# Attention decode on one core: the softmax bias moves from POOL to ACT, and PSUM buffers and program order are rearranged

## The chip, the cores and the metric

The kernel runs on 1 core of one Trainium2 chip. The metric is the device time of one execution in microseconds (us), given as the median of several executions. One that takes over 1.5% more than the fastest of its kernel is counted as slow.

Engines: PE is TensorE (PEld its weight loads), DVE is VectorE, ACT is ScalarE, POOL is GpSimd, SP issues the DMAs.

## The reference

Two decode attention blocks, A and B, with one query position, 4 batches, 32 query heads, 8 K/V heads of 128 and a model width of 512. A attends to 4096 keys, B to the last 1024.

```python
q = (x @ wq).reshape(B, Sq, Hq, Dh).transpose(0, 2, 1, 3)
scores = einsum("bhqd,bhkd->bhqk", q, repeat(k, 4)) * (Dh ** -0.5)
p = softmax(scores)
o = einsum("bhqk,bhkd->bhqd", p, repeat(v, 4))
out = o.transpose(0, 2, 1, 3).reshape(B, Sq, Hq * Dh) @ wo
# the results of A and B are concatenated
```

All inputs are bf16. The caches that are used make 84 MB and the weights 17 MB; the core reads 100.67 MB in all.

## The kernel before

The work is cut into 40 units, each with 1 MB of K and 1 MB of V: 32 units for A (one K/V head, one batch, 4096 keys) and 8 for B (one K/V head, four batches, 1024 keys). In a unit

1. PE transposes K in 32 blocks of 128x128 into PSUM, 8 blocks to a bank, and DVE copies each bank to SBUF (K copies);
2. PE makes the scores (32 matmuls with 4 columns), DVE takes the maximum of each partition;
3. POOL takes the maximum over the partitions (an all-reduce, tile bm) and multiplies it by -scale (tile biasT);
4. ACT takes exp(scale * s + biasT); DVE sums each partition, POOL sums over the partitions (an all-reduce, tile den);
5. PE multiplies with V (PV); DVE normalises; after each group of heads PE adds its part of the output projection.

The POOL program before:

```python
for t in range(self.NU):
    ...
    self.wait(g_, f"dve.red.{t}")
    ... g_.partition_all_reduce(self.bm[:, s, 0:w], self.pm[:, s, 0:w], 128, max)
    self.inc(ins, "pool", f"pool.max.{t}")
    self.wait(g_, f"pool.max.{t}")
    ...
    g_.tensor_scalar(out=self.biasT[:, s, 0:w], in0=self.bm[:, s, 0:w],
                     scalar1=-self.scale, scalar2=None, op0=ALU.mult)
    self.inc(ins, "pool", f"pool.bias.{t}")
    if t - self.Ld >= 0:
        self._pool_den(g_, t - self.Ld)     # waits for dve.rsum, all-reduce (add) den<-acc
```

ACT waits for `pool.bias` and for the scores. The order of one step on PE and on DVE, cut to its core:

```python
# PE, step t                         # DVE, step t
transposes(t + 1)                    kcopies(t + LK)        # LK = 2
scores(t)                            reduce_max(t)
pv(t - 2)                            rowsum(t - 1)
outproj(...)                         norm(t - 1)            # waits for pool.den and pv
```

The transposes use two PSUM banks in turn, so group j waits for the K copy of group j - 2. SP issues the loads in program order: K three units ahead of V.

Of the kernel before, what the change touches and what calls it, by code (L numbers as in the profile page):

```python
# [7 lines left out]
ACT_F = mybir.ActivationFunctionType  # L8
ALU = mybir.AluOpType
AX = mybir.AxisListType  # L10

F32 = mybir.dt.float32
# [3 lines left out]
    NK=3,  # L16
# [5 lines left out]
    LT=1,  # L22
    LK=2,
    La=1,
    Ld=1,
    NE=4,
    NY=4,
# [3 lines left out]
    wo1_at=22,  # L31
    KLEAD=3,
)


class _Builder:
    def __init__(self, nc, aps, cfg):
        self.nc = nc
        self.aps = aps
        self.cfg = cfg  # L40
        self.rec = None
        self.NB = 4
        self.DM = 512
        self.HQ = 32
        self.HKV = 8
        self.REP = 4
        self.DH = 128
        self.SK = 4096
        self.W = min(4096, max(256, self.SK // 4))
        self.C = [self.SK // 128, self.W // 128]  # L50
        self.KOFF = [0, self.SK - self.W]
        self.KEYS = [self.SK, self.W]
        self.scale = 1.0 / math.sqrt(float(self.DH))
        self.NK = cfg["NK"]
        self.NV = cfg["NV"]
        self.NRD = cfg["NRD"]
        self.NRA = cfg["NRA"]
        self.NPS = cfg["NPS"]
        self.L = cfg["L"]
        self.LT = cfg["LT"]  # L60
        self.LK = cfg["LK"]
        self.La = cfg["La"]
        self.Ld = cfg["Ld"]
        self.NE = cfg["NE"]
        self.NY = cfg["NY"]
        self.NR = self.NRD + self.NRA
        assert self.L < self.NPS and self.L < self.NE and self.La < self.L and self.Ld <= self.La
        self.LO = max(self.L, self.La + self.LK + 1)
        self.units = []
        for g in range(self.HKV):  # L70
            for b in range(self.NB):
                self.units.append((0, g, b, 1))
        self.NUA = len(self.units)
        for g in range(self.HKV):
            self.units.append((1, g, 0, self.NB))
        self.NU = len(self.units)
        self.Q = 32
        for (P, g, b0, nb) in self.units:
            assert nb * self.C[P] == self.Q
        self.groups = []  # L80
        j = 0
        for t in range(self.NU):
            glist = []
            for q0 in range(0, self.Q, 8):
                glist.append((j, q0, 8))
                j += 1
            self.groups.append(glist)
        self.QB0 = cfg["QB0"]
        assert self.QB0 >= self.L and self.QB0 + self.NPIECE + self.L < self.NUA
# [60 lines left out]
    def _issue_k(self, eng, t):  # L150
        em = self.emit
        P, g, b0, nb, C = self.uinfo(t)
        off = self.KOFF[P]
        r = t % self.NR
        if r >= self.NRD:
            self.wait(eng, "pe.q.0")
        if t - self.NR >= 0:
            self.wait(eng, f"pe.tlast.{t - self.NR}")
        ins = None
        if em:  # L160
            src = self.k_cache[P][b0:b0 + nb, g, off:off + C * 128, :].rearrange(
                "b (p c) d -> p b c d", p=128
            )
            dst = self.Rq(r).rearrange("p (b c) d -> p b c d", b=nb)
            ins = eng.dma_start(dst, src)
        self.op("dma", self.Q * 128 * 128 * 2)
        self.inc(ins, f"dmakr{r}", f"dma.k.{t}", 16)
# [59 lines left out]
    def prog_pool(self, g_):  # L227
# [32 lines left out]
        for t in range(self.NU):  # L260
# [4 lines left out]
            if t - NY >= 0:  # L265
                self.wait(g_, f"pool.bias.{t - NY}")
            ins = (
# [7 lines left out]
            self.inc(ins, "pool", f"pool.max.{t}")  # L275
            self.wait(g_, f"pool.max.{t}")
            if t - NY >= 0:
                self.wait(g_, f"act.exp.{t - NY}.last")
            ins = (
                g_.tensor_scalar(  # L280
                    out=self.biasT[:, s, 0:w], in0=self.bm[:, s, 0:w],
                    scalar1=-self.scale, scalar2=None, op0=ALU.mult,
                )
                if em
                else None
            )
            self.op("pool.tscalar")
            self.inc(ins, "pool", f"pool.bias.{t}")
            if t - self.Ld >= 0:
# [57 lines left out]
    def _act_exps(self, act, i):  # L347
# [5 lines left out]
        kb = i % self.NPS  # L353
        self.wait(act, f"pool.bias.{i}")
        self.wait(act, f"pe.s.{i}")
# [21 lines left out]
    def prog_pe(self, pe):  # L377
# [21 lines left out]
        for step in range(self.NU + LO):  # L399
            t = step  # L400
            if t + LT < self.NU:
                self._pe_transposes(pe, t + LT)
            if t < self.NU:
                self._pe_scores(pe, t)
            i = step - L
            if 0 <= i < self.NU:
                k = step - self.QB0
                if 0 <= k < self.NPIECE:
                    self._pe_qTB_chunk(pe, i, k)
                self._pe_pv(pe, i)  # L410
            i = step - LO
            if 0 <= i < self.NU:
# [24 lines left out]
    def _pe_qTB_chunk(self, pe, i, k):  # L437
        em = self.emit
        ob = i % self.NOT
        self.qb_chunk_of_unit[i] = k  # L440
# [4 lines left out]
        self.wait(pe, "dve.xcopy")  # L445
        if i - self.NOT >= 0:
            self.wait(pe, f"dve.mult.{i - self.NOT}")
        reg = self.oTt[ob][:, 16 + 16 * k:32 + 16 * k].rearrange("p (j bb) -> p j bb", j=4)
        for jj in range(4):
# [17 lines left out]
    def _pe_transposes(self, pe, t):  # L467
        em = self.emit
        P, g, b0, nb, C = self.uinfo(t)
        r = t % self.NR  # L470
        self.wait(pe, f"dma.k.{t}")
        for (j, q0, ng) in self.groups[t]:
            kb = j % 2
            if j - 2 >= 0:
                self.wait(pe, f"dve.kcopy.{j - 2}")
            for k in range(ng):
# [12 lines left out]
    def _pe_scores(self, pe, t):  # L489
# [3 lines left out]
        kb = t % self.NPS  # L493
        self.wait(pe, f"dve.kcopy.{self.groups[t][-1][0]}")
        KTv = self.KTq(s)
        self.wait(pe, f"dve.qcopy.{P}")
        if t - self.NPS >= 0:
            self.wait(pe, f"act.exp.{t - self.NPS}.last")
            self.wait(pe, f"dve.red.{t - self.NPS}")
        ps = self.psT[kb][:, 0:self.Q * 4].rearrange("p (q h) -> p q h", h=4)  # L500
        for b in range(nb):
            qT = self.qT_sb[P][:, b0 + b, self.REP * g:self.REP * g + 4]
            for c in range(C):
                q = b * C + c
                ins = None
                if em:
                    ins = pe.matmul(ps[:, q, :], lhsT=KTv[:, q, :], rhs=qT, start=True, stop=True)  # L507
                self.op("pe.mm4s")
                if q == self.Q - 1:
                    self.inc(ins, "pe_s", f"pe.s.{t}")  # L510

    def _pe_pv(self, pe, i):
# [3 lines left out]
        se = i % self.NE  # L516
        ob = i % self.NOT
        self.wait(pe, f"dma.v.{i}")
        self.wait(pe, f"act.exp.{i}.last")
        if i - self.NOT >= 0:  # L520
            self.wait(pe, f"dve.mult.{i - self.NOT}")
        if i in self.qb_chunk_of_unit:
# [38 lines left out]
    def prog_dve(self, dve):  # L561
# [17 lines left out]
        for step in range(self.NU + La):  # L579
# [3 lines left out]
            if t < self.NU:  # L583
                self._dve_reduce(dve, t)
            i_q = step + LK - self.L - 1
            if i_q in self.qb_chunk_of_unit:
                assert i_q <= step - La, "qT_B chunk copy must precede norm of its unit"
                self._dve_qbcopy(dve, i_q, self.qb_chunk_of_unit[i_q])
# [29 lines left out]
    def _dve_kcopies(self, dve, t):  # L618
        em = self.emit
        P, g, b0, nb, C = self.uinfo(t)  # L620
        s = t % self.NK
        if t - self.NK >= 0:
            self.wait(dve, f"pe.s.{t - self.NK}")
        dst = self.KTq(s)
        for (j, q0, ng) in self.groups[t]:
            kb = j % 2
            self.wait(dve, f"pe.tgrp.{j}")
# [38 lines left out]
    def _dve_qbcopy(self, dve, i, k):  # L666
        em = self.emit
        ob = i % self.NOT
        self.wait(dve, f"pe.qb.{k}")
        ins = None  # L670
        if em:
            ins = dve.tensor_copy(
                self.qT_sb[1][:, :, 4 * k:4 * k + 4].rearrange("p bb j -> p j bb"),
                self.oTt[ob][:, 16 + 16 * k:32 + 16 * k].rearrange("p (j bb) -> p j bb", j=4),
            )
# [5 lines left out]
    def _dve_norm(self, dve, i):  # L681
        em = self.emit
        P, g, b0, nb, C = self.uinfo(i)
        sy = i % self.NY
        ob = i % self.NOT
        w = nb * 4
# [22 lines left out]
    def build(self):  # L709
# [9 lines left out]
        with contextlib.ExitStack() as stack:  # L719
# [29 lines left out]
            self.OT_all = [sb(f"OT_all{P}", [128, self.HQ, self.NB], BF16) for P in range(2)]  # L749
            self.out_sb = sb("out_sb", [128, 2, self.DM], BF16)  # L750
            self.psT = [pb(f"psT{k}", [128, 512], F32) for k in range(self.NPS)]
            self.NOT = 8 - self.NPS - 3
            assert self.NOT >= 1
            self.oTt = [pb(f"oT{k}", [128, 512], F32) for k in range(self.NOT)]
            self.oT = [t[:, 0:16] for t in self.oTt]
            self.outp = pb("outp", [128, self.DM], F32)
            self.KTps_t = [pb(f"KTps{k}", [128, 512], F32) for k in range(2)]
            self.KTps = [t[:, :].bitcast(BF16).rearrange("p (c k) -> p c k", c=8)
# [14 lines left out]
            names += [f"dmav{s}" for s in range(NV)]  # L773
            names += [f"dmakr{r}" for r in range(NRD + NRA)]
            for n in names:
                self._new_sem(n)
# [83 lines left out]
```

## Time and profile before

| | before |
|---|---|
| median of 15 runs | 802.79 us (799.23 to 806.29) |
| span of the profiled run | 805.4 us |
| busiest compute engine | PE, 31% of the span |
| DMA queue | 33.7% of 16 engines' span |
| POOL, idle on "issue" before biasT and den | 332.3 + 236.3 us |

Part 1 of the profile page of the kernel before is the busy time of each engine, with its share of the span:

```profile
PE 248.5 (31%) x4168; PEld 213.9 (27%) x4168; DVE 137.3 (17%) x332; ACT 50.1 (6%) x257; POOL 44.5 (6%) x128
```

No engine is anywhere near full. Such a page suggests that something waits in series, and one has to look for who waits for whom. The view of the waits (engine and line that waits, releaser, us in total, times, longest):

```profile
ACT e_sb L365 <- POOL biasT L280: 716.4, 40, 22.3
DVE rden L692 <- POOL den L304: 601.3, 40, 25.1
PE KTps L479 <- DVE KT L630: 490.6, 37, 23.6
```

ACT and DVE wait for POOL, PE waits for DVE. POOL is the head of the queue although it is busy for only 6%. The groups of POOL instructions tell the rest (busy us, mean ns of one, then the idle time just before them and what ended it):

```profile
L304 POOL PARTITION_ALL_REDUCE den<-acc x40 | 17.7, 442 | 237.1 <-issue 236.3 <-DVE acc L662 0.8
L268 POOL PARTITION_ALL_REDUCE bm<-pm x40 | 15.4, 385 | 177.5 <-DVE pm L646 169.4 <-issue 8.1
L280 POOL TENSOR_SCALAR biasT<-bm 128x4 f32<-128x4 f32 (+1 forms) x40 | 10.5, 263 | 332.3 <-issue 332.3
```

"issue" is idle time in which the engine waited for nothing that the profile shows. POOL stands still for 568.6 us before biasT and den, with no other engine to blame. In order of time it looks like this (start, us, engine, line, instruction, idle before it):

```profile
319.07 0.44 POOL L304 PARTITION_ALL_REDUCE den<-acc  x1 [5.84 <-issue]
323.49 0.38 POOL L268 PARTITION_ALL_REDUCE bm<-pm  x1 [3.98 <-DVE pm L646]
331.47 0.26 POOL L280 TENSOR_SCALAR biasT<-bm 128x4 f32<-128x4 f32 x1 [7.60 <-issue]
337.70 0.44 POOL L304 PARTITION_ALL_REDUCE den<-acc  x1 [5.97 <-issue]
...
798.38 0.44 POOL L304 PARTITION_ALL_REDUCE den<-acc  x1 [5.93 <-issue]
799.61 0.44 POOL L304 PARTITION_ALL_REDUCE den<-acc  x1 [0.79 <-DVE acc L662]
```

The all-reduce bm follows another all-reduce and starts as soon as DVE is done. The tensor_scalar, which follows an all-reduce, and the all-reduce den, which follows the tensor_scalar, have 6 to 8 us of nothing before them. The last two den follow each other with no multiply between them, and the gap is not there.

### The profile page before, as it was taken

What the parts mean: (1) busy time and instruction counts of PE and PEld (TensorE: products, weight loads), DVE (VectorE), ACT (ScalarE), POOL (GpSimd) and SP (SyncE); (2) the same over time, 40 slices, a digit from 0 to 9 for tenths busy, and PEclk for the clock granted to TensorE, in tenths of its full rate; (3) what the DMA queues carried; (4) which work ended last, traced back from release to release, by engine and by line L of the source; (5) the groups of instructions that cost most, each with busy time, mean ns of one, the idle gap of its engine ahead of it and who ended that gap; (6) DMA issues with size and microseconds to landing.
All of it is one profiled execution on the core that took longest, in us unless ns stands there. A gap on an engine that the chain in (4) does not pass through costs nothing.

```text
span 805.4 us, 9583 instructions
## 1 busy us (share of the span) xinstructions
PE 248.5 (31%) x4168; PEld 213.9 (27%) x4168; DVE 137.3 (17%) x332; ACT 50.1 (6%) x257; POOL 44.5 (6%) x128
## 2 busy tenths in 40 slices
PE   1712222322232224333322332232223222333323
PEld 1712222222222223332222222222222222222201
DVE  0501111111111112211111111111111111111100
ACT  0000000000000000000000000000000001112111
POOL 0000000000000000000000000000000000000000
PEclk9955555555555555555555555555555555555555
DMA  8995444332222222222523333433233221110000
GB/s 354 392 407 189 172 171 169 131 104 106 105 105 105 105 105 105 105 105 91 205 106 137 133 142 135 142 110 111 99 127 110 107 78 52 53 53 1 1 1 1
DMA packets 27867, 101.31 MB, mean 126 GB/s; under 512 B 1696, under 2 KB 9904, under 8 KB 19120
## 3 DMA queue, kind: packets, MB, share of 16 engines
q1 hardware_dynamic: 27824, 100.69, 33.7%
q8 instruction: 33, 0.54, 0.3%
q14 instruction: 10, 0.08, 0.0%
HBM read 100.67 MB, written 0.01 MB: 125 GB/s over the span
## 4 chain that ended last, share of the span: by engine, by line
issue 88%; POOL 5%; PE 3%; DMA 2%; DVE 1%; POOLq 1%; SPq 0%; ACT 0%
POOL den L304 2%; POOL bm L268 2%; DMA rawKd<-in_A_k_cache_dram 2%; PE KTps L479 2%; POOL biasT L280 1%; PE outp L550 0%; PE psT L426 0%; DVE KT L630 0%; POOLq L280 0%; POOLq L304 0%; PE psT L507 0%; ACT e_sb L365 0%; DVE out_sb L614 0%; DVE rden L692 0%; DVE pm L646 0%
## 5 line engine op out<-in xcount | busy, mean ns | idle before, releaser
L479 PE MATMUL KTps<-ident,rawKd 128*128 128x128 bf16 x896 | 103.2, 307 | 325.0 <-DVE KT L630 317.3
L479 PEld LDWEIGHTS KTps<-ident,rawKd 128*128 128x128 bf16 x896 | 88.9, 143 | 339.3 <-DVE KT L630 324.3
L630 DVE COPY KT<-KTps 128x1024 bf16<-128x1024 bf16 x160 | 106.7, 686 | 36.9 <-PE KTps L479 36.6
L692 DVE RECIPROCAL rden<-den 128x4 f32<-128x4 f32 (+1 forms) x40 | 7.7, 193 | 601.3 <-POOL den L304 601.3
L479 PE MATMUL KTps<-ident,big_w 128*128 128x128 bf16 x384 | 45.1, 312 | 173.3 <-DVE KT L630 173.3
L365 ACT ACTIVATE e_sb<-psT,biasT 128x32 bf16<-128x32 f32 (+1 forms) x256 | 48.8, 329 | 716.4 <-POOL biasT L280 716.4
L479 PEld LDWEIGHTS KTps<-ident,big_w 128*128 128x128 bf16 x384 | 39.0, 145 | 178.2 <-DVE KT L630 176.5
L529 PE MATMUL oT<-e_sb,V 128*128 128x4 bf16 x1280 | 39.7, 166 | 45.8 <-ACT e_sb L365 42.5
L529 PEld LDWEIGHTS oT<-e_sb,V 128*128 128x128 bf16 x1280 | 37.3, 104 | 48.1 <-issue 48.1
L507 PEld LDWEIGHTS psT<-qT_sb,KT 128*128 128x128 bf16 x1280 | 41.9, 106 | 0.9 <-issue 0.9
L507 PE MATMUL psT<-qT_sb,KT 128*128 128x4 bf16 x1280 | 41.3, 167 | 0.0
L304 POOL PARTITION_ALL_REDUCE den<-acc x40 | 17.7, 442 | 237.1 <-issue 236.3
L280 POOL TENSOR_SCALAR biasT<-bm 128x4 f32<-128x4 f32 (+1 forms) x40 | 10.5, 263 | 332.3 <-issue 332.3
L268 POOL PARTITION_ALL_REDUCE bm<-pm x40 | 15.4, 385 | 177.5 <-DVE pm L646 169.4
L550 PE MATMUL outp<-big_w,OT_all 128*4 128x512 bf16 x32 | 14.8, 622 | 1.4 <-DVE OT_all L699 1.4
L550 PE MATMUL outp<-wo_sb,OT_all 128*4 128x512 bf16 x32 | 14.9, 620 | 0.0
L662 DVE TENSOR_REDUCE acc<-e_sb 128x4 f32<-128x128 bf16 (+1 forms) x40 | 11.1, 277 | 9.3 <-ACT e_sb L365 9.3
L646 DVE TENSOR_REDUCE pm<-psT 128x4 f32<-128x128 f32 (+1 forms) x40 | 11.2, 281 | 0.0
L699 DVE TENSOR_TENSOR OT_all<-oT,rden 128x4 bf16<-128x4 f32 (+1 forms) x40 | 6.9, 173 | 1.4
L550 PEld LDWEIGHTS outp<-big_w,OT_all 128*4 128x4 bf16 x32 | 2.9, 108 | 7.8 <-issue 5.1
L454 PE MATMUL oT<-xT_sb,big_w 128*128 128x4 bf16 x128 | 4.5, 166 | 0.0
L454 PEld LDWEIGHTS oT<-xT_sb,big_w 128*128 128x128 bf16 x128 | 4.0, 104 | 0.0
(18 smaller groups left out, 17.1 us busy)
## 6 DMA issues: line engine op xcount, KB each, us to landing
V<-in_A_v_cache_dram SPq DMA_DIRECT2D x32, 1024.0 KB, 5.1
rawKd<-in_A_k_cache_dram SPq DMA_DIRECT2D x22, 1024.0 KB, 8.3
big_w<-in_A_k_cache_dram SPq DMA_DIRECT2D x10, 1024.0 KB, 7.7
V<-in_B_v_cache_dram SPq DMA_DIRECT2D x8, 1024.0 KB, 5.3
rawKd<-in_B_k_cache_dram SPq DMA_DIRECT2D x6, 1024.0 KB, 7.7
big_w<-in_A_wq_dram SPq DMA_DIRECT2D x1, 4096.0 KB, 12.5
big_w<-in_B_wq_dram SPq DMA_DIRECT2D x8, 512.0 KB, 12.3
wo_sb<-in_A_wo_dram SPq DMA_DIRECT2D x8, 512.0 KB, 10.9
```

Source lines behind the costliest of these rows:

```text
L268: g_.partition_all_reduce(self.bm[:, s, 0:w], self.pm[:, s, 0:w], 128, bass.bass_isa.ReduceOp.max)
L280: g_.tensor_scalar(out=self.biasT[:, s, 0:w], in0=self.bm[:, s, 0:w], scalar1=-self.scale, scalar2=None, op0=ALU.mult,)
L304: g_.partition_all_reduce(self.den[:, s, 0:w], self.acc[:, s, 0:w], 128, bass.bass_isa.ReduceOp.add)
L365: ins = act.activation(self.e_sb[:, se, b * C:(b + 1) * C, h], ps[:, b * C:(b + 1) * C, h], ACT_F.Exp, bias=self.biasT[:, sy, idx:idx + 1] ...
L454: ins = pe.matmul(reg[:, jj, :], lhsT=self.wq_sb[1][:, kc, j * 128:(j + 1) * 128], rhs=self.xT_sb[:, 1, kc, :], start=(kc == 0), stop=(kc ...
L479: ins = pe.transpose(self.KTps[kb][:, k, :], self.Rq(r)[:, q0 + k, :], self.ident128[:, :],)
L507: ins = pe.matmul(ps[:, q, :], lhsT=KTv[:, q, :], rhs=qT, start=True, stop=True)
L529: ins = pe.matmul(self.oT[ob][:, b * 4:(b + 1) * 4], lhsT=self.Vq(s)[:, q, :], rhs=self.e_sb[:, se, q, :], start=(c == 0), stop=(c == C - 1),)
L550: ins = pe.matmul(self.outp[0:self.NB, :], lhsT=self.OT_all[P][:, h, :], rhs=self.wo_sb[P][:, h, :], start=(h == 0), stop=(h == self.HQ - 1),)
L630: ins = dve.tensor_copy(dst[:, q0:q0 + ng, :], self.KTps[kb][:, 0:ng, :])
L646: ins = dve.reduce_max(self.pm[:, sy, 0:w], ps, axis=AX.X)
L662: ins = dve.reduce_sum(self.acc[:, sy, 0:w], ev, axis=AX.X)
```

## The change

The diff has four intents: to take the multiply off POOL and give it to ACT; to double the PSUM banks of the transposes (two to four), paid for by putting the PV result into spare columns of the score banks; to run PV before the scores and K copies one unit ahead instead of two; and to prepare a path that lets the DMA transpose K, which is left empty (`XBAR_UNITS=()`). The core of the diff:

```diff
-    LK=2,
+    LK=1,
+    NKTB=4,
+    XBAR_UNITS=(),
 ... POOL program
-            self.wait(g_, f"pool.max.{t}")
-            ...
-                g_.tensor_scalar(
-                    out=self.biasT[:, s, 0:w], in0=self.bm[:, s, 0:w],
-                    scalar1=-self.scale, scalar2=None, op0=ALU.mult,
-                )
-            self.inc(ins, "pool", f"pool.bias.{t}")
 ... ACT program
-        self.wait(act, f"pool.bias.{i}")
+        self.wait(act, f"pool.max.{i}")
+            act.activation(
+                self.biasT[:, sy, 0:nb * 4], self.bm[:, sy, 0:nb * 4],
+                ACT_F.Copy, scale=-self.scale,
+            )
+        self.inc(ins, "act", f"act.bias.{i}")
+        self.wait(act, f"act.bias.{i}")
 ... PE program: the scores move behind PV
-            if t < self.NU:
-                self._pe_scores(pe, t)
             i = step - L
             if 0 <= i < self.NU:
                 ...
                 self._pe_pv(pe, i)
+            if t < self.NU:
+                self._pe_scores(pe, t)
 ... transposes
-            kb = j % 2
-            if j - 2 >= 0:
-                self.wait(pe, f"dve.kcopy.{j - 2}")
+            kb = j % self.NKTB
+            if j - self.NKTB >= 0:
+                self.wait(pe, f"dve.kcopy.{j - self.NKTB}")
 ... PSUM
-            self.oTt = [pb(f"oT{k}", [128, 512], F32) for k in range(self.NOT)]
-            self.oT = [t[:, 0:16] for t in self.oTt]
+            self.oT = [t[:, 128:144] for t in self.psT]
 ... (the waits and the q_B columns that follow from this are cut)
```

## The prediction

> **What bounds the kernel now.** No engine is busy over 31% of the span (page, part 1: PE 248.5 us, DVE 137.3, ACT 50.1, POOL 44.5 of 805.4); the DMA queue has 33.7% (part 3). The chain of waits is 88% "issue", between POOL instructions. The groups of instructions show where: before the 40 tensor_scalar (biasT) POOL idles 332.3 us on "issue", 8.3 us each, and before the all-reduces den 236.3 us, 6.1 us each, though their inputs are ready. Before the all-reduce bm there is no such gap (timeline: it starts 0.1 us after the row maximum it waits for), and the last two all-reduces den follow each other without one. So an all-reduce is really 0.4 us, and the gap appears where POOL changes between the all-reduce and an ordinary instruction, both ways. [...] the other direction costs more, 11 us while DMA is full. A unit takes 17.6 to 20 us; 14.4 of it are these two changes.
>
> **What the change does.** The -scale multiply moves from POOL to ACT. POOL then runs only all-reduces: both changes go, 569 us, all on the chain. ACT gets 40 small activations, an estimated 0.2 to 0.3 us each (an exp is 0.22); ACT has 0.87 us of work in an A unit and 2.64 in a B unit, so this is off the path. I expect no further table loads.
> The rest (four transpose buffers, LK=1, oT in the score banks, PV before scores) frees PE from waiting on DVE copies two groups back. The cross-bar path is empty and does nothing.
>
> **What bounds it then.** 805 - 569 = 236 us is below two floors:
> - DMA: 100.69 MB. Windows with a full queue show 393 to 428 GB/s; at 400, 252 us, plus a slow first 5 us and a tail of about 8 us: 262 to 268.
> - PE: 248.5 us at mostly half clock, starting at 17 us, plus the tail: 271, more with gaps. An A unit is 3.8 (32 transposes at 118 ns) + 1.04 + 0.99 + 0.47 = 6.3 us at half clock against 5.2 us of DMA. At 32 us the trace shows transposes at 66 ns after dense PE work; then a unit is about 4.3 us and DMA bounds. [...]
> - DVE: 3.7 us a unit, below both.
>
> Early units also carry 8.4 MB of weights, so are DMA-bound; later ones start PE-bound and should warm the clock. I expect 272 us, range 257 to 300.
>
> **What would show it.** POOL "issue" idle gone (under 20 us in all), all-reduces still 0.38 to 0.44 us; DMA share 9 tenths in most slices, 380 to 410 GB/s; PE mean clock well above 0.54; a unit every 5.2 to 6.3 us; PE's largest waits on K or V loads, not on DVE.
>
> **What would make it wrong.** The gap could belong to each all-reduce, or max and add could need different code: about 6 us a unit would stay, 450 us or more. Copy and Exp could alternate table loads (1.28 us each): up to 100 us on ACT, partly hidden. The clock could stay at half and PE, DVE and POOL hand over in series: 300 us or more. [...]
>
> Chances: faster by over 2% 0.98, within 2% 0.01, slower 0.01.

Two phrases have these numbers in the trace of the kernel before: in the "slow first 5 us" the queue moved 154 GB/s, against 418 in the next 5; and that later units "should warm the clock" is the author's estimate from the transposes, which took 66 ns each at 32.7 us, behind dense PE work, and 117 ns each at 46.5 us, at a granted clock of 0.50.

## The result, and the profile after

The changed kernel takes 269.54 us (median of 8 runs, 268.27 to 270.02), against 802.79 us. The ratio is 0.3356, with a 95% interval of 0.3349 to 0.3363. Ratios here are the mean time of one kernel's fast runs over that of the other's of the same rounds, so they are not quite the ratio of the medians.

Part 1 of the page, two rows of part 2 (the span in 40 slices: granted PE clock and busy DMA, in tenths) and the DMA queue of part 3, of the changed kernel:

```profile
PE 218.1 (81%) x4168; PEld 191.1 (71%) x4168; DVE 130.4 (49%) x332; ACT 58.3 (22%) x297; POOL 32.6 (12%) x88
...
PEclk9997997757755557757555756897797777759956
DMA  6999999999999999999999999999999999999810
...
q1 hardware_dynamic: 27824, 100.69, 95.3%
```

The DMA queue, 33.7% before, is now full in 36 consecutive slices. PE does the same 4168 matmuls in less busy time; its mean granted clock rose from 0.536 to 0.733 in the two profiled runs.

The groups of POOL instructions of the changed kernel, and then a stretch of its POOL timeline:

```profile
L319 POOL PARTITION_ALL_REDUCE den<-acc x40 | 19.6, 489 | 24.2 <-DVE acc L692 24.2
L296 POOL PARTITION_ALL_REDUCE bm<-pm x40 | 15.0, 374 | 196.7 <-DVE pm L676 196.7
```

```profile
158.85 0.37 POOL L296 PARTITION_ALL_REDUCE bm<-pm  x1 [4.34 <-DVE pm L676]
159.13 0.50 POOL L319 PARTITION_ALL_REDUCE den<-acc  x1
163.99 0.37 POOL L296 PARTITION_ALL_REDUCE bm<-pm  x1 [4.36 <-DVE pm L676]
```

"issue" is gone before both all-reduces; POOL now waits for DVE, as it should. The all-reduces last about as long as before (bm 374 ns against 385, den 489 against 442). A unit takes about 5 us, 163.99 - 158.85 = 5.14 here. What ACT got, in its groups:

```profile
L371 ACT ACTIVATE biasT<-bm 128x4 f32<-128x4 f32 (+1 forms) x40 | 8.4, 210 | 200.7 <-POOL bm L296 200.7
L371 ACT ACT_TABLE_LOAD x1 | 1.3, 1283 | 0.7 <-PEq L876 0.7
```

The multiply costs ACT 8.4 us in all. There is still one table load in the whole program (1.28 us): Copy beside Exp causes none. The waits of PE in the changed kernel:

```profile
PE KTps L505 <- DMA rawKd<-in_A_k_cache_dram: 16.2, 5, 7.6
PE KTps L505 <- DMA big_w<-in_A_k_cache_dram: 5.3, 2, 2.8
PE KTps L505 <- DVE KT L660: 5.1, 14, 1.5
```

PE waited 490.6 us for DVE's K copies before. It now waits 5.1 us for them, and most of what is left in these lines is for K loads.

### The profile page after: what moved, and what is told of

Its sections match the earlier page's. It is cut to its first block, busy times and chain, and to the rows that moved or that the text cites. A ratio compares the mean times of both kernels' runs of the same rounds, so it can differ in the third digit from the quotient of the medians.

```text
span 268.2 us, 9433 instructions
## 1 busy us (share of the span) xinstructions
PE 218.1 (81%) x4168; PEld 191.1 (71%) x4168; DVE 130.4 (49%) x332; ACT 58.3 (22%) x297; POOL 32.6 (12%) x88
## 4 chain that ended last, share of the span: by engine, by line
PE 55%; DMA 29%; DVE 7%; SPq 4%; issue 3%; ACT 1%; POOL 0%; DVEq 0%
PE KTps L505 32%; DMA rawKd<-in_A_k_cache_dram 23%; PE psT L558 9%; PE outp L579 6%; DMA big_w<-in_B_k_cache_dram 6%; PE psT L538 5%; DVE KT L660 4%; SPq L210 1%; PE psT L478 1%; PE psT L451 1%; SPq L237 1%; ACT e_sb L390 1%; SPq L251 1%; DVE OT_all L729 1%; DVE qT_sb L702 1%
## 5 line engine op out<-in xcount | busy, mean ns | idle before, releaser
L660 DVE COPY KT<-KTps 128x1024 bf16<-128x1024 bf16 x160 | 99.5, 681 | 9.5 <-PE KTps L505 9.5
L505 PE MATMUL KTps<-ident,rawKd 128*128 128x128 bf16 x896 | 82.7, 272 | 22.6 <-DMA rawKd<-in_A_k_cache_dram 16.2
L505 PEld LDWEIGHTS KTps<-ident,rawKd 128*128 128x128 bf16 x896 | 75.1, 126 | 32.2 <-issue 16.3
L371 ACT ACTIVATE biasT<-bm 128x4 f32<-128x4 f32 (+1 forms) x40 | 8.4, 210 | 200.7 <-POOL bm L296 200.7
L558 PEld LDWEIGHTS psT<-e_sb,V 128*128 128x128 bf16 x1280 | 38.1, 100 | 8.2 <-issue 7.7
L558 PE MATMUL psT<-e_sb,V 128*128 128x4 bf16 x1280 | 39.4, 166 | 5.1 <-DVE acc L692 3.3
L505 PE MATMUL KTps<-ident,big_w 128*128 128x128 bf16 x384 | 36.6, 275 | 7.7 <-DMA big_w<-in_A_k_cache_dram 5.3
L505 PEld LDWEIGHTS KTps<-ident,big_w 128*128 128x128 bf16 x384 | 32.8, 128 | 11.4 <-DMA big_w<-in_A_k_cache_dram 5.4
L538 PEld LDWEIGHTS psT<-qT_sb,KT 128*128 128x128 bf16 x1280 | 36.1, 98 | 3.5 <-issue 3.3
L729 DVE TENSOR_TENSOR OT_all<-psT,rden 128x4 bf16<-128x4 f32 (+1 forms) x40 | 6.9, 174 | 59.3 <-PE psT L558 59.1
```

Of the source, the lines that this page charges most:

```text
L371: act.activation(self.biasT[:, sy, 0:nb * 4], self.bm[:, sy, 0:nb * 4], ACT_F.Copy, scale=-self.scale,)
L505: ins = pe.transpose(self.KTps[kb][:, k, :], self.Rq(r)[:, q0 + k, :], self.ident128[:, :],)
L538: ins = pe.matmul(ps[:, q, :], lhsT=KTv[:, q, :], rhs=qT, start=True, stop=True)
L558: ins = pe.matmul(self.oT[ob][:, b * 4:(b + 1) * 4], lhsT=self.Vq(s)[:, q, :], rhs=self.e_sb[:, se, q, :], start=(c == 0), stop=(c == C - 1),)
L660: ins = dve.tensor_copy(dst[:, q0:q0 + ng, :], self.KTps[kb][:, 0:ng, :])
L729: ins = dve.tensor_tensor(self.OT_all[P][:, self.REP * g:self.REP * g + 4, b0:b0 + nb].rearrange("p h b -> p b h"), self.oT[ob][:, 0:w].re ...
```

## The experiments

Theory A: POOL pays some 6 us or more each time it goes from an all-reduce to the multiply or back, and the whole gain is that these changes are gone. Rivals: the other edits carry part of the gain; the all-reduce itself hides the time; or what cost was the dependence, max, multiply and exp in series through POOL. Theory D: the changed kernel is bound by DMA, not by PE. "Code", which POOL changes or needs in the prediction and the expectations, is the author's guess at what such a gap is; the traces show the gap and its length, not what POOL does in it.

The yardstick was run again in two of the calls: 269.89 us (ratio 0.3334) and 269.79 us (ratio 0.3326). Its ratio moves because the kernel before, on those chips, took 810.7 and 810.37 us. The runs e2 to e6 rest on two executions each, the others on four or five.

> The changed kernel unaltered, as the yardstick for the other runs of this call: 268 to 271 us.

> The changed kernel unaltered, as the yardstick for the other run of this call: 268 to 271 us.

### Only the multiply moves (e1_bias_only)

```diff
 # the kernel before, and of the whole change only this:
-                g_.tensor_scalar(out=self.biasT..., in0=self.bm..., scalar1=-self.scale, ...)
+            act.activation(self.biasT..., self.bm..., ACT_F.Copy, scale=-self.scale)
-        self.wait(act, f"pool.bias.{i}")
+        self.wait(act, f"pool.max.{i}")
```

> The kernel before with only the -scale multiply moved from POOL to ACT (two transpose buffers, LK=2, own oT banks, scores before PV, all as before). Theory A, the whole gain is the two changes of code on POOL: 265 to 300 us, near the changed kernel. Rival B, the other edits (four transpose buffers, order of PV and scores) are needed to use what POOL sets free: over 330 us.

Measured: 271.63 us, ratio 0.3355 (0.3335 to 0.3374); the full change had 0.3334 (0.332 to 0.3348). The moved multiply alone is the gain, to within 2 us. Everything else in the diff is worth 0.6% here by the two ratios, and as their intervals overlap even that is not certain.

### Everything but the multiply (e2_rest_only)

```diff
 # the changed kernel, with the multiply back on POOL
+                g_.tensor_scalar(out=self.biasT..., in0=self.bm..., scalar1=-self.scale, ...)
-            act.activation(self.biasT..., self.bm..., ACT_F.Copy, scale=-self.scale)
```

> The changed kernel with the -scale multiply put back on POOL, all other edits kept. Theory A, the gain is all in the multiply leaving POOL: 770 to 810 us. Rival B, the other edits bring a good part by themselves: under 720 us.

Measured: 750.56 us, ratio 0.9326 (0.9215 to 0.9438). Neither expectation held: the other edits do gain while POOL bounds, 54 us by the medians. The POOL groups of this run:

```profile
L332 POOL PARTITION_ALL_REDUCE den<-acc x40 | 17.7, 442 | 255.0 <-issue 254.3 <-DVE acc L695 0.8
L296 POOL PARTITION_ALL_REDUCE bm<-pm x40 | 15.4, 385 | 144.0 <-DVE pm L679 135.6 <-issue 8.4
L308 POOL TENSOR_SCALAR biasT<-bm 128x4 f32<-128x4 f32 (+1 forms) x40 | 10.5, 263 | 292.7 <-issue 292.7
```

Against the kernel before, POOL waits 169.4 - 135.6 = 33.8 us less for DVE's maximum. From den to the next bm, DVE normalises, copies four K banks and takes the maximum; with two banks it had to wait for PE in the midst of the four copies (3.98 us in the timeline before), with four banks the transposes are already there (3.10 us in the timeline of this run). Another 21.6 us are shorter "issue" (332.3 + 236.3 before, 292.7 + 254.3 here); the spans of the two profiled runs differ by 55.3 us. Why those gaps became shorter was not tested. They vary within a run too: in the kernel before, the one before the tensor_scalar is 10.88 and 11.10 us at 44 and 64 us, while the DMA queue is full (412 and 398 GB/s in these two gaps), and mostly 7 to 9 us later. The gain of these edits and that of the multiply don't add: once POOL is free, DMA bounds, and the 54 us have nowhere to show.

### A multiply that nobody needs (e3_one_scalar, e4_four_scalars)

```diff
 # the changed kernel, in each unit between the two all-reduces; input constant, result unused
+            for k in range(1):          # e4: range(4)
+                g_.tensor_scalar(out=self.scr[:, s, k, 0:4], in0=self.cst[:, 0:4],
+                                 scalar1=-self.scale, scalar2=None, op0=ALU.mult)
```

> The changed kernel plus one tensor_scalar of 128x4 on POOL in each unit, between the two all-reduces; its input is a constant and nobody waits for its result. Theory A, POOL pays for changing between the all-reduce and an ordinary instruction, whatever depends on it: 700 to 810 us, with about 6 us before each following all-reduce and 6 to 9 us before each tensor_scalar. Rival, it was the dependence (max, multiply, exp in series) that cost: 268 to 280 us.

> As the run with one extra tensor_scalar per unit, but four in a row. Theory A, the cost is per change of code: the same gaps once per unit, so at most 35 us (3 x 40 x 0.26 us and a little) above the run with one. Rival, the cost is per ordinary instruction: three times 6 us and more per unit on top, over 1300 us.

Measured: 746.26 us with one and 774.07 us with four (ratios 0.9273 and 0.9619). One unused instruction of 0.26 us per unit costs 476 us, so the dependence is not what cost. Three more of them cost only 28 us, nearly all of it their own busy time (36.9 us instead of 10.3), so the price is not per instruction either. The POOL timeline with one, then with four:

```profile
152.81 0.26 POOL L311 TENSOR_SCALAR scr<-cst 128x4 f32<-128x4 f32 x1 [6.93 <-issue]
159.13 0.44 POOL L334 PARTITION_ALL_REDUCE den<-acc  x1 [6.06 <-issue]
162.67 0.38 POOL L299 PARTITION_ALL_REDUCE bm<-pm  x1 [3.10 <-DVE pm L691]
```

```profile
154.15 1.16 POOL L311 TENSOR_SCALAR scr<-cst 128x4 f32<-128x4 f32 x4 [7.60 <-issue]
161.35 0.44 POOL L334 PARTITION_ALL_REDUCE den<-acc  x1 [6.04 <-issue]
```

There is one gap into the group of multiplies and one out of it, whether the group has one or four.

### A memset in its place (e6_one_memset)

```diff
+            g_.memset(self.scr[:, s, k, 0:4], 0.0)      # instead of the tensor_scalar
```

> As the run with one extra tensor_scalar per unit, but a memset of 128x4 in its place. If every ordinary instruction makes POOL change its code: 700 to 810 us. If the change is needed for tensor_scalar and not for memset (at the start of the kernel the first memset ran at once, the first affine_select 7.85 us later): 268 to 275 us. I lean to the first, 60 to 40.

Measured: 269.74 us (two runs), ratio 0.3352 (0.331 to 0.3394): nothing is lost. My lean was wrong. The POOL timeline:

```profile
154.41 0.37 POOL L299 PARTITION_ALL_REDUCE bm<-pm  x1 [3.66 <-DVE pm L688]
154.65 0.17 POOL L311 MEMSET scr<- 128x4 f32 x1
154.72 0.50 POOL L331 PARTITION_ALL_REDUCE den<-acc  x1
```

A memset between two all-reduces has no gap on either side. So not every "ordinary instruction" costs: the tensor_scalar does, the memset doesn't. No other kind was tried in the loop.

The trace of the kernel before names something at these gaps: pairs of MODIFY_POOL_CONFIG on POOL's sequencer (POOLq). They are not counted as busy time, so POOL looks idle there. In the view of a source line (`--source`), first two lines of the kernel before, then two of the changed kernel (count, then ns min/median/max):

```profile
L280 POOLq MODIFY_POOL_CONFIG  x80: 83/85/88, 33.5 to 784.5; - x80
L304 POOLq MODIFY_POOL_CONFIG  x78: 11/11/11, 64.8 to 792.8; - x78
L262 POOLq MODIFY_POOL_CONFIG  x2: 11/11/11, 1.0 to 1.1; - x2
L296 POOLq MODIFY_POOL_CONFIG  x2: 13/13/13, 9.6 to 9.6; - x2
```

With two more pairs at the line of bm and one at the start, 164 of these records stand in the trace of the kernel before (805.4 us) and 4 in that of the changed kernel (268.2 us), at 1.0 and 9.6 us. In the loop of the kernel before that is 40 pairs for the tensor_scalar, 39 for den and one for bm, which has the 8.1 us of "issue" in its line. 332.3 + 236.3 + 8.1 = 576.7 us over these 80 is 7.2 us each. A pair itself is short (11 to 88 ns a record); 6.6 to 11.0 us pass from the end of a pair to the tensor_scalar, and 5.5 to 7.1 us to den. In e3 two POOLq records stand at the same place, 0.31 us behind the tensor_scalar and 5.71 us before den. What fills these microseconds is not shown: the queue for instructions moved 33 packets and 0.54 MB in the kernel before and in the changed one alike, so no extra transfer is seen there.

### More all-reduces (e5_four_allreduces)

```diff
+            for k in range(4):
+                g_.partition_all_reduce(self.scr[:, s, k, 0:4], self.cst[:, 0:4], 128, max)
```

> The changed kernel plus four more all-reduces (max, 128x4, constant input, nobody waits) in each unit, between the two of the kernel. Theory A, an all-reduce costs what its record shows: about 2 us more on POOL per unit of about 6 us, and den and bias come up to 2 us later: 268 to 280 us, no gaps on POOL. Rival, an all-reduce hides 6 us of its own: over 1000 us.

Measured: 272.47 us, ratio 0.3393 (0.3370 to 0.3415). The 160 extra all-reduces keep POOL busy for 60.4 us and cost the kernel some 3 us. The POOL timeline of one unit:

```profile
152.95 0.37 POOL L299 PARTITION_ALL_REDUCE bm<-pm  x1 [3.38 <-DVE pm L690]
153.22 1.51 POOL L311 PARTITION_ALL_REDUCE scr<-cst  x4
154.64 0.51 POOL L333 PARTITION_ALL_REDUCE den<-acc  x1
```

Max after max and add after max follow without a gap. An all-reduce hides no gap of its own.

### What bounds the changed kernel (e8_half_pv, e7_half_v)

```diff
 # e8: every second PV matmul only (wrong result on purpose)
-            for c in range(C):
+            for c in range(0, C, 2):
 # e7: half of each V load, PV uses that half twice (wrong result on purpose)
+            src = ...[:, :, 0:C // 2, :];  dst = ...[:, :, 0:C // 2, :]
-                        lhsT=self.Vq(s)[:, q, :],
+                        lhsT=self.Vq(s)[:, b * C + c % (C // 2), :],
```

> The changed kernel with only every second PV matmul (a wrong result on purpose), same loads; 640 matmuls of about 30 ns issue each are gone, some 20 us of PE work. Theory D, DMA bounds the changed kernel: 264 to 270 us, at most the tail gets shorter. Rival P, PE bounds it: about 20 us less, 250 us.

> The changed kernel with only half of each V load (a wrong result on purpose), all PE work kept: 21 MB of 100.7 MB less, 52 us at 400 GB/s. Theory D, DMA bounds the changed kernel: clearly shorter, 217 us if nothing else steps in; I expect 220 to 240, because PE has 218 us of work at its mixed clock and starts at 17 us. Rival P, PE bounds it: 262 to 270 us.

Measured: 268.07 us without half of the PV matmuls (ratio 0.331, 0.3297 to 0.3323, against 0.3334) and 247.65 us without half of V (ratio 0.3073, 0.3048 to 0.3098). (One of the four runs of e7, 249.94 us, was slow; the fast three have a median of 247.34 us, and the ratio is theirs.) Taking 17 us of PE's busy time away (200.7 us against 217.9) brings under 2 us; taking loads away brings 22 us. So DMA bounds. But 21 MB at 400 GB/s are 52 us, and only 22 came: 247.65 us is above the 220 to 240 us that I expected. Part 1 of e7 and its DMA row:

```profile
PE 204.6 (83%) x4168; PEld 182.8 (74%) x4168; DVE 130.5 (53%) x332; ACT 58.3 (24%) x297; POOL 32.6 (13%) x88
...
DMA  5999999999999999999983799999999999532000
```

With less to load, the DMA queue runs short once in the middle and drains well before the end. PE, busy 83% of the span although it starts at about 17 us, is probably the next limit; no run took PE work out of e7 to show it. If so, DMA and PE lie within some 22 us of each other in the changed kernel.

### Trying to shorten the end (e9_k_earlier, e10_short_tail)

In the changed kernel, the DMA queue thins out from about 250 us on (269 GB/s to 254 us, 122 to 258, 2 after) and PE works until 266 us. Two versions were to shorten this end.

```diff
 # e9: K loads run further ahead of V from unit 24 on
+            lead = KL + (t >= 24) + (t >= 28)
+            while kn <= t + lead and kn < self.NU:
+                self._issue_k(sp, kn); kn += 1
 # e10: projection one step sooner; weights before x; last maximum before the last K copies
-        self.LO = max(self.L, self.La + self.LK + 1)
+        self.LO = self.L
 ...
```

> The changed kernel with the K loads issued up to two units further ahead of the V loads from unit 24 on (same loads, other order). The DMA queue is idle in the last 14 us of the changed kernel while transposes, scores, exps and PV of the last units run. Theory T, that tail hangs on the last K loads coming late: 3 to 7 us less, 262 to 266 us. Rival, the tail is the rate of PE, DVE and ACT over the last units: within 1 us of the changed kernel.

> The changed kernel with three small edits of its two ends, loads and work the same: the projection of a unit is issued one step sooner (LO=2), the first weight load is issued before the two small x loads, and in the step before the last DVE takes the row maximum before the K copies. The DMA queue stays the bound, so only the ends can move: about 1.4 us from the projection, 1 us from the maximum, under 0.7 us from the first load: 2 to 3.5 us less than the changed kernel, about 267 us. Rival, the end is set by PE work in series at its half clock, which these edits only move: within 1 us.

e9 took 274.18 us, ratio 0.3388 (0.3372 to 0.3404) against 0.3334: 1.6% slower, where theory T expected 3 to 7 us less. The waits of PE in this run:

```profile
PE KTps L508 <- DMA rawKd<-in_A_k_cache_dram: 16.4, 6, 7.5
PE psT L561 <- DMA V<-in_A_v_cache_dram: 10.0, 6, 4.4
```

PE waits as long for K as before (16.2), and now 10.0 us for V of A, against 0.2 us in the changed kernel (1.5 us in its run of the same call). The queue was full there (385 to 402 GB/s from 180 to 250 us), so an earlier K was a later V, and PE, which takes PV and transposes in program order, stopped for either.

e10 took 269.36 us, ratio 0.3326 (0.3313 to 0.3339) against 0.3326 (0.3316 to 0.3337): the same, as its rival said. With the projection one step sooner, each of the last three projections stands directly behind its own PV and the normalisation, and waits for it:

```profile
256.81 1.86 PE L579 MATMUL outp<-big_w,OT_all 128*4 128x512 bf16 x4 [0.23 <-DVE OT_all L732]
258.61 1.01 PE L558 MATMUL psT<-e_sb,V 128*128 128x4 bf16 x32
259.98 1.87 PE L579 MATMUL outp<-big_w,OT_all 128*4 128x512 bf16 x4 [0.36 <-DVE OT_all L732]
```

So e10 only moved the work at the end, which is PE, DVE and ACT in series at a granted clock of 0.67 from 250 to 260 us and 0.50 after, and e9 made PE wait for V. No version that beats the changed kernel was found.

## Why the prediction was right

- **What bounded the kernel before: right.** POOL's 569 us of "issue" before biasT and den were the bound. One unused tensor_scalar per unit brings the changed kernel back to 746.26 us (e3).
- **The reason: right in place, too wide in its words.** The prediction said that the gap appears where POOL changes "between the all-reduce and an ordinary instruction". A memset is ordinary and causes no gap (e6). It is the tensor_scalar against the all-reduce, two changes in each unit, each with a MODIFY_POOL_CONFIG pair (80 in the loop of the kernel before). In the lines above they cost 5.8 to 6.1 us before den and 6.9 to 7.6 us before the tensor_scalar.
- **The all-reduce is really 0.4 us: right** (e5, 0.37 to 0.51 us).
- **The multiply on ACT, 0.2 to 0.3 us and no further table load: right,** 0.21 us and one load.
- **805 - 569 = 236 us is below the floor of DMA: right.** The gain was cut off by DMA. Halving V shortens the kernel, halving PV hardly does (e7, e8).
- **Size of the floor: 252 us for the bytes held, the tail was too short.** The full slices show 379 to 428 GB/s and the queue still carried 122 GB/s between 254 and 258 us. After the queue thins out, the rest takes some 13 us, not 8: PV, exps and two projections of the last units run in series, at a mean granted clock of 0.62 from 258 us on. That is the difference between the 262 to 268 us of this floor and the 269.54 us measured. The forecast of 272 was above it because it leaned towards the PE floor of 271, which took 248.5 us of PE work; at the clock that PE got it was 218.1 us. One floor was too low and the other too high, so it is partly luck that 272 came within 2.5 us.
- **PE's granted clock rises and DMA stays the bound: right,** with a mean of 0.733 after 0.536 and a unit of about 5 us. PE did not stay at the full clock; it was between half and full in 31 of 40 slices. The transposes show it too: in the changed kernel 32 of them took 3.57 us at 23.3 us, 1.95 us (61 ns each) at 27.5 us, 3.43 us at 225 us and 1.96 us at 245 us. In the kernel before, 32 took 3.67 us (115 ns each) at 28.4 us and 16 took 1.05 us (66 ns each) at 32.7 us, while the record of the granted clock reads 1.00 from the start to 38 us; so that record does not show this step, and what brings it was not tested.
- **"The rest ... frees PE from waiting on DVE copies": not borne out.** With the multiply moved and two buffers kept (e1), PE waits 5.6 us for K copies, against 5.1 us in the changed kernel; with four buffers and the multiply on POOL (e2) it waits 445.6 us. These waits went with the multiply. The rest gives 54 us while POOL bounds (e2) and at most 2 us after (e1).

## What to carry to other kernels

When no engine is busy and the waits lead to an engine that idles on "issue", look at which pairs of instructions have the gap between them: the cost can belong to the alternation and not to either instruction, and here the cure was to take one of the two off that engine. Look at the engine's sequencer too (POOLq): there the change had a name, and a count, 164 records in the trace of the kernel before and 4 in that of the changed one. Ask before sizing a gain which floor stands below it: here 569 us of removed idle time would have gone to 236 us, and the loads stop it at 270. Once a load queue is full, issuing one stream earlier can make the other later (in e9, 10.0 us of waits for V of A instead of 0.2).
